# Retention by feature in column tiles, and one product for x by token and the logits

## The chip, the cores and the metric

The kernel runs on one core of one Trainium2 chip. The metric is device time in microseconds (us) of that core. The profile is one execution recorded by the hardware profiler; times inside it count from the first instruction. The engines are PE (TensorE matmul; PEld is its weight load), DVE (VectorE), ACT (ScalarE), POOL (GpSimd) and SP (SyncE, which here only issues transfers).

## What is computed

Retention over 8 sequences of 576 tokens with 8 heads of 64 features, then a mixture of 8 experts in which a local gate can keep the expert of the token before. All data is 32-bit floating point.

```python
scores = scale * np.matmul(q, k.transpose(0, 1, 3, 2))            # q, k, v: (8, 8, 576, 64)
gamma = 1.0 - 2.0 ** (-5.0 - np.arange(H))
Dmat = np.where(rel >= 0, gamma[:, None, None] ** rel[None], 0.0) # rel = query place - key place
x = np.matmul(scores * Dmat, v)                                   # then (B, S, H*D) = (8, 576, 512)
logits = x @ w_gate;  local_gate = sigmoid(x @ w_local)
for each sequence, for each token s:
    e = argmax(logits[s]) if s == 0 or local_gate[s] < 0.5 else the expert of token s - 1
    out[s] = softmax(logits[s])[e] * (relu(x[s] @ w1[e]) @ w2[e]) # w1: (8, 512, 1024), w2: (8, 1024, 512)
```

## The kernel before

**Three stages.** Retention turns q, k and v into x, 128 tokens (a *chunk*) at a time, writes x to DRAM and keeps the logits of both gates. Routing works out on all 4608 tokens which expert each goes to and which slot it gets. The experts' stage gathers x by slot, 256 slots to a block, and sends 25 blocks through their expert's weights. Routing needs the logits of every token, and the address of the first expert's weights needs the routing, so the stages follow one another.

**A chunk of retention.** Two sequences of 576 tokens are nine chunks; the fifth (`m == MID`) ends one sequence and begins the next. The decay is split into a factor by query place and one by key place, so a chunk needs only a triangular mask and a running 64 x 64 state per head. `scores(i)` loads the chunk (`ld`, L107: queries by feature, keys and values by token), transposes the keys on PE (`kps`, L112), copies them on ACT (`kT`, L114), scales the values by key decay on POOL (`vs`, L116), multiplies keys and queries per head (`sps`, L123) and masks the result on DVE (`sT`, L127). The products of L123 have 64 rows of contraction: even heads use partitions 0 to 63, odd heads 64 to 127, in turn. `outputs(i)` adds up in `ops` the chunk's own part (L139, 8 products) and the state's (L146, 4 products), brings the state up to date (`kv` on PE, L155, copied to `state` by ACT, L161), scales `ops` by query decay on DVE (`x`, L163) and stores x (L166). `logits(i)` transposes x (`xps`, L172), copies it on ACT (`xT`, L174) and multiplies it with the gates' weights into `lps` (L176), which is copied once at the end of the stage (`lt`, L187).

**What sets the order.** The program is written as a pipeline: chunk i + 1's scores, chunk i's outputs, chunk i - 1's logits. A scheduler orders each engine's instructions when the program is built, and so the groups of one chunk on PE stand among those of its neighbours. Tiles come from pools with a fixed number of buffers (`raw` 4, `work` 3, `ps_s` 3, `ps_t` 2, `ps_o` and `ps_kv` 1): a tile waits until the reader of the one whose buffer it takes is done. SP issues the loads and the stores of x in its own order; two small tables come over ACT's queue at the start. On PE a 32-bit product is carried out as two passes, each a weight load and a matmul, and shows as two instructions in the profile; a transpose is one.

Of the kernel before, what the change touches and what calls it, by code (L numbers as in the profile page):

```python
# [9 lines left out]
F32 = mybir.dt.float32  # L10
# [9 lines left out]
P = 128  # L20
# [21 lines left out]
def kernel(  # L42
# [3 lines left out]
    decay: bass.AP,  # L46
# [25 lines left out]
    with ExitStack() as part:  # L72
# [26 lines left out]
        lps = ps_l.tile([P, NCH, E + 1], F32, name="lps")  # L99
        chunks = [{} for _ in range(NCH)]  # L100
        kv = None

        def scores(i):
            m = i % PER
            g = chunks[i]
            ld = raw.tile([P, 3, D], F32, name="ld")
            nc.sync.dma_start(out=ld.rearrange("p t x -> p (t x)"), in_=qkv[i])  # L107
            qT = ld[:, 0].rearrange("p (c s) -> p c s", c=HP)
            kn, vn = ld[:, 1], ld[:, 2]
            kps = ps_t.tile([P, HP, P], F32, name="kps", tag="t")  # L110
            for c in range(HP):
                nc.tensor.transpose(kps[:, c, :], kn[:, c * P:(c + 1) * P], ident)  # L112
            kT = work.tile([P, HP, P], F32, name="kT")
            nc.scalar.copy(kT, kps)  # L114
# [3 lines left out]
                dec[:, 1, m, :].unsqueeze(2).to_broadcast([P, H, DH]), op=Alu.mult)  # L118
            sps = [ps_s.tile([P, HP, P], F32, name=f"sps{u}", tag="s") for u in range(2)]
            for c in range(HP):  # L120
                for u in range(2):
                    r = slice(u * DH, (u + 1) * DH)
                    nc.tensor.matmul(sps[u][:, c, :], lhsT=kT[r, c, :], rhs=qT[r, c, :],  # L123
                                     start=True, stop=True, skip_group_check=True)
# [332 lines left out]
```

## Time and profile before

| What | Value |
|---|---|
| Runs | median 1039.18 us of 3 (1037.77 to 1045.94) |
| Profiled execution, first to last instruction | 1037.5 us (its own time is this span; the median of the runs is 1.7 us above it) |
| Busy, share of the span | PE 94%, PEld 69%, DVE 16%, POOL 14%, ACT 12% |
| Granted TensorE clock, mean | 0.977 |
| DMA | 166 MB, 160 GB/s over the span |
| Retention | until 250.83 us, when `lt` is copied |
| Routing | until about 274 us |
| Experts | until the end |

A profile row of the time line has start and busy time in us, the engine, the kernel's line, the operation, output <- inputs, for PE the active rows * columns of the array and the shape of the output, and how many instructions are merged in the row. In a row by group, the numbers after the bar are the sum of busy time in us, the mean of one instruction in ns, and the idle time ahead of the group with what ended it. Matmuls are pipelined: one lasts some 280 ns though the next starts well before that, so what a pass costs is read from start to start.

### The profile page before, as it was taken

Reading aid. Unit: us, or ns where it says so; the run is one execution under the profiler, and the core shown is the slowest. Engines: PE = TensorE matmul, PEld = TensorE weight load, DVE = VectorE, ACT = ScalarE, POOL = GpSimd, SP = SyncE. Lnnn points to the kernel's source line nnn. Section 1 sums busy time; section 2 is a strip of 40 time slices with the busy share of each in tenths; the row PEclk is TensorE's granted clock in tenths of the full one; section 3 lists DMA queues with packets and bytes.
Section 4 is the critical chain, followed back from the end, with each engine's and each line's share of the span. In section 5 each row is a group of like instructions: output and inputs, shape, how many; then the busy total and the mean of one; then the engine's idle time right before and its main releaser. Section 6 shows DMA issues by size and latency. Waiting matters only on the chain. (4 is left out here: it accounts for less than half of the span.)

```text
span 1037.5 us, 12062 instructions
## 1 busy us (share of the span) xinstructions
PE 974.9 (94%) x4918; PEld 719.0 (69%) x4918; DVE 166.8 (16%) x282; ACT 123.8 (12%) x238; POOL 140.7 (14%) x158
## 2 busy tenths in 40 slices
PE   7999999996479999999999999999999999999995
PEld 6999999995466666666666666666666666666662
DVE  2333332324711111010111111010111110010100
ACT  2222222221000000000000000000000000000000
POOL 2111111110021111011111110011111110110000
PEclk9999999998589999999999999999999999999998
DMA  5444444430735544555455544555455544555300
GB/s 201 154 158 157 151 163 162 163 133 32 273 122 203 201 156 148 185 197 177 153 179 187 193 156 153 181 193 188 138 187 203 164 158 160 195 183 167 127 2 0
DMA packets 47509, 166.03 MB, mean 160 GB/s; under 512 B 7006, under 2 KB 7134, under 8 KB 47456
## 3 DMA queue, kind: packets, MB, share of 16 engines
q1 hardware_dynamic: 39168, 142.62, 40.5%
q0 software_dynamic: 8000, 22.56, 6.3%
q8 instruction: 39, 0.64, 0.2%
q14 instruction: 14, 0.11, 0.0%
q10 hardware_dynamic: 288, 0.09, 0.0%
HBM read 146.37 MB, written 22.54 MB: 163 GB/s over the span
## 5 line engine op out<-in xcount | busy, mean ns | idle before, releaser
L395 PE MATMUL hps<-xTs,w1s 128*128 128x256 f32 x1600 | 353.2, 382 | 14.1 <-DVE xTs L389 14.1
L402 PE MATMUL yps<-w2s,hT 128*128 128x512 f32 x800 | 347.4, 592 | 0.0
L395 PEld LDWEIGHTS hps<-xTs,w1s 128*128 128x128 f32 x1600 | 303.0, 191 | 60.2 <-DVE xTs L389 19.8
L402 PEld LDWEIGHTS yps<-w2s,hT 128*128 128x128 f32 x800 | 152.0, 190 | 180.7 <-issue 179.4
L405 DVE TENSOR_SCALAR y<-yps,pslot 128x512 f32<-128x512 f32 x50 | 37.5, 751 | 665.4 <-PE yps L402 665.4
L397 ACT ACTIVATE hT<-hps 128x512 f32<-128x512 f32 x100 | 59.7, 597 | 700.2 <-PE hps L395 700.2
L406 POOL DMA_INDIRECT out_dram<-y,sidx x50 | 50.7, 1014 | 512.0 <-DVE y L405 505.3
L139 PE MATMUL ops<-vs,sT 128*128 128x64 f32 x576 | 82.3, 277 | 0.0
L139 PEld LDWEIGHTS ops<-vs,sT 128*128 128x128 f32 x576 | 72.4, 191 | 4.9 <-issue 0.6
L127 DVE TENSOR_TENSOR sT<-sps,mask 128x512 f32<-128x512 f32 x72 | 46.4, 686 | 159.9 <-PE sps L123 159.9
L383 POOL DMA_INDIRECT xg<-xd,gidx x50 | 48.7, 975 | 164.0 <-PE xgps L388 121.2
L116 POOL TENSOR_TENSOR vs<-ld,dec 128x512 f32<-128x512 f32 x36 | 37.5, 1042 | 190.0 <-PE kv L155 173.2
L123 PE MATMUL sps<-ld,kT 64*128 64x128 f32 x576 | 43.2, 288 | 0.2 <-DVE sT L127 0.2
L161 ACT COPY state<-kv 64x256 f32<-64x256 f32 x64 | 23.4, 366 | 160.2 <-PE kv L155 159.4
L176 PE MATMUL lps<-wg,xT 128*128 128x9 f32 x288 | 38.0, 259 | 1.5 <-ACT xT L174 1.1
L176 PEld LDWEIGHTS lps<-wg,xT 128*128 128x128 f32 x288 | 34.9, 191 | 5.2 <-ACT xT L174 4.7
L123 PEld LDWEIGHTS sps<-ld,kT 64*128 64x128 f32 x576 | 36.3, 190 | 2.9 <-DVE sT L127 0.4
L388 PEld LDWEIGHTS xgps<-ident,xg 128*128 128x128 f32 x200 | 24.2, 146 | 20.1 <-issue 19.5
L155 PE MATMUL kv<-vs,ld 128*128 128x128 f32 (+1 forms) x256 | 35.5, 281 | 0.5 <-ACT state L161 0.5
L146 PE MATMUL ops<-state,ld 128*128 128x128 f32 (+1 forms) x256 | 35.4, 281 | 0.0
L388 PE MATMUL xgps<-ident,xg 128*128 128x128 f32 x200 | 27.7, 282 | 6.6 <-DMA xg<-xd,gidx 6.6
L389 DVE COPY xTs<-xgps 128x512 f32<-128x512 f32 x50 | 32.2, 682 | 7.1 <-PE xgps L388 7.1
(112 smaller groups left out, 271.2 us busy)
## 6 DMA issues: line engine op xcount, KB each, us to landing
w1s<-in_w_dram SPq DMA_DIRECT2D x100, 512.0 KB, 5.5
w2s<-in_w_dram SPq DMA_DIRECT2D x100, 512.0 KB, 8.1
ld<-in_qkv_dram SPq DMA_DIRECT2D x36, 768.0 KB, 4.5
xd<-x SPq DMA_DIRECT2D x36, 256.0 KB, 2.2
xg<-xd,gidx POOLq DMA_INDIRECT x50, 7.3
out_dram<-y,sidx POOLq DMA_INDIRECT x50, 7.5
dec<-in_decay_dram ACTq DMA_DIRECT2D x1, 72.0 KB, 4.6
wg<-in_wgl_dram ACTq DMA_DIRECT2D x1, 18.0 KB, 6.2
```

Source lines behind the costliest of these rows:

```text
L116: nc.gpsimd.tensor_tensor(vs.rearrange("p (h d) -> p h d", h=H), vn.rearrange("p (h d) -> p h d", h=H), dec[:, 1, m, :].unsqueeze(2).to_br ...
L123: nc.tensor.matmul(sps[u][:, c, :], lhsT=kT[r, c, :], rhs=qT[r, c, :], start=True, stop=True, skip_group_check=True)
L127: nc.vector.tensor_tensor(sT[:, u], sps[u], (mask2 if m == MID else mask).unsqueeze(1).to_broadcast([P, HP, P]), op=Alu.mult)
L139: nc.tensor.matmul(ops[:, h, :], lhsT=sT[:, h % 2, h // 2, :], rhs=vs[:, h * DH:(h + 1) * DH], start=(h == 0), stop=(m == 0), skip_group_c ...
L176: nc.tensor.matmul(lps[:, i, :], lhsT=xT[:, c, :], rhs=wg[:, c, :], start=(c == 0), stop=(c == DK - 1), skip_group_check=True)
L383: nc.gpsimd.indirect_dma_start(out=xg, out_offset=None, in_=xd, in_offset=bass.IndirectOffsetOnAxis(ap=gidx[:, s:s + 1], axis=0))
L388: nc.tensor.transpose(xps[:, c, :], xg[:, c * P:(c + 1) * P], ident)
L395: nc.tensor.matmul(hps[:, v, :], lhsT=w1s[:, m + v, c, :], rhs=xT[:, c, :], start=(c == 0), stop=(c == DK - 1), skip_group_check=True)
L397: nc.scalar.activation(hT[:, m:m + 2, :], hps, Act.Relu)
L402: nc.tensor.matmul(yps, lhsT=hT[:, m, u * P:(u + 1) * P], rhs=w2s[:, m, :], start=(m == 0), stop=(m == FK - 1))
L405: nc.vector.tensor_scalar(y, yps, pslot[:, s:s + 1], None, Alu.mult)
L406: nc.gpsimd.indirect_dma_start(out=out, out_offset=bass.IndirectOffsetOnAxis(ap=sidx[:, s:s + 1], axis=0), in_=y, in_offset=None, bounds_c ...
```

## The change

`ops` is computed the other way round, by feature instead of by token: the values are the stationary operand with 64 columns, the masked scores stream, and even and odd heads write partitions 0 to 63 and 64 to 127, that is, they use the left and the right 64 columns of the array (L163 of the changed kernel). The state's part of `ops` is turned round in the same way (L144). `kv` is computed per head in 64 columns each instead of per pair of heads in 128 (L154), without the products between different heads, which were thrown away. x therefore comes out by feature (`xT`, L168, scaled by a table of query decay by feature and place, `decq`, of 1280 KB instead of a small one). One product per 128 features with the matrix [identity, gates' weights] (`gates`, 137 columns) then gives x by token and that part of the logits at once (`nps`, L175); ACT copies x out (L178), DVE sums the logits' four parts into `lt` (L179), and x is stored (L181). Keys are loaded in both layouts, so that `ld` grows from 768 to 1024 KB and their transposes and copies go.

```diff
-        ps_t = pool(part, "ps_t", 2, PSUM)
         ps_s = pool(part, "ps_s", 3, PSUM)
-        ps_o = pool(part, "ps_o", 1, PSUM)
+        ps_o = pool(part, "ps_o", 2, PSUM)
+        ps_n = pool(part, "ps_n", 1, PSUM)
         ps_kv = pool(part, "ps_kv", 1, PSUM)
-        ps_l = pool(part, "ps_l", 1, PSUM)
...
-        dec = once.tile([P, 2, PER, H], F32, name="dec")
-        nc.scalar.dma_start(out=dec.rearrange("p t m h -> p (t m h)"), in_=decay)
-        wg = once.tile([P, DK, E + 1], F32, name="wg")
-        nc.scalar.dma_start(out=wg.rearrange("p k e -> p (k e)"), in_=wgl)
+        deck = once.tile([P, PER, H], F32, name="deck")
+        nc.scalar.dma_start(out=deck.rearrange("p m h -> p (m h)"), in_=decay_k)
+        gates = once.tile([P, DK, P + E + 1], F32, name="gates")
+        nc.scalar.dma_start(out=gates[:, :, P:], in_=wgl.rearrange("p (k e) -> p k e", k=DK))
+        decq = once.tile([P, HP, S + HALF], F32, name="decq")
+        nc.scalar.dma_start(out=decq.rearrange("p c s -> p (c s)"), in_=decay_q)
+        for c in range(DK):
+            nc.gpsimd.tensor_copy(gates[:, c, 0:P], ident)
...
+        def half(u):
+            return slice(u * DH, (u + 1) * DH)
...
         def scores(i):
-            ld = raw.tile([P, 3, D], F32, name="ld")
+            ld = raw.tile([P, 4, D], F32, name="ld")
             nc.sync.dma_start(out=ld.rearrange("p t x -> p (t x)"), in_=qkv[i])
             qT = ld[:, 0].rearrange("p (c s) -> p c s", c=HP)
-            kn, vn = ld[:, 1], ld[:, 2]
-            kps = ps_t.tile([P, HP, P], F32, name="kps", tag="t")
-            for c in range(HP):
-                nc.tensor.transpose(kps[:, c, :], kn[:, c * P:(c + 1) * P], ident)
-            kT = work.tile([P, HP, P], F32, name="kT")
-            nc.scalar.copy(kT, kps)
+            kT = ld[:, 1].rearrange("p (c s) -> p c s", c=HP)
+            kn, vn = ld[:, 2], ld[:, 3]
...
         def outputs(i):
-            ops = ps_o.tile([P, H, DH], F32, name="ops")
-            for h in range(H):
-                nc.tensor.matmul(ops[:, h, :], lhsT=sT[:, h % 2, h // 2, :],
-                                 rhs=vs[:, h * DH:(h + 1) * DH],
-                                 start=(h == 0), stop=(m == 0), skip_group_check=True)
+            ops = ps_o.tile([P, HP, P], F32, name="ops")
             if m > 0:
                 n = HALF if m == MID else P
                 for c in range(HP):
-                    nc.tensor.matmul(
-                        ops[0:n, 2 * c:2 * c + 2, :].rearrange("p h d -> p (h d)"),
-                        lhsT=qT[:, c, 0:n], rhs=states[(i + 1) % 2][:, c, :],
-                        start=False, stop=True, skip_group_check=True)
+                    nc.tensor.matmul(ops[:, c, 0:n], lhsT=states[(i + 1) % 2][:, c, :],
+                                     rhs=qT[:, c, 0:n], start=(c == 0), stop=False,
+                                     skip_group_check=True)
             if m != PER - 1:
                 r = slice(HALF, P) if m == MID else slice(0, P)
                 if m in (0, MID):
-                    kv = ps_kv.tile([P, HP, P], F32, name="kv")
+                    kv = ps_kv.tile([P, HP, DH], F32, name="kv")
                 for c in range(HP):
-                    nc.tensor.matmul(kv[:, c, :], lhsT=kn[r, c * P:(c + 1) * P],
-                                     rhs=vs[r, c * P:(c + 1) * P],
-                                     start=(m in (0, MID) and c == 0), stop=True,
-                                     skip_group_check=True)
+                    for u in range(2):
+                        h = 2 * c + u
+                        nc.tensor.matmul(kv[half(u), c, :], lhsT=kn[r, h * DH:(h + 1) * DH],
+                                         rhs=vs[r, h * DH:(h + 1) * DH],
+                                         start=(m in (0, MID) and c == 0), stop=True,
+                                         skip_group_check=True)
                 for u in range(2):
-                    r = slice(u * DH, (u + 1) * DH)
-                    nc.scalar.copy(states[i % 2][r, :, r], kv[r, :, r])
-            g["x"] = x = work.tile([P, D], F32, name="x")
-            nc.vector.tensor_tensor(
-                x.rearrange("p (h d) -> p h d", h=H), ops,
-                dec[:, 0, m, :].unsqueeze(2).to_broadcast([P, H, DH]), op=Alu.mult)
-            nc.sync.dma_start(out=xd[i * P:(i + 1) * P, :], in_=x)
+                    nc.scalar.copy(states[i % 2][half(u), :, half(u)], kv[half(u)])
+            for c in range(HP):
+                for u in range(2):
+                    h = 2 * c + u
+                    nc.tensor.matmul(ops[half(u), c, :], lhsT=vs[:, h * DH:(h + 1) * DH],
+                                     rhs=sT[:, u, c, :], start=(m == 0 and c == 0), stop=True,
+                                     skip_group_check=True)
+            g["xT"] = xT = work.tile([P, HP, P], F32, name="xT")
+            at = (m * P) % S
+            nc.vector.tensor_tensor(xT, ops, decq[:, :, at:at + P], op=Alu.mult)
...
-        def logits(i):
-            x = chunks[i]["x"]
-            xps = ps_t.tile([P, DK, P], F32, name="xps", tag="t")
-            for c in range(DK):
-                nc.tensor.transpose(xps[:, c, :], x[:, c * P:(c + 1) * P], ident)
-            xT = work.tile([P, DK, P], F32, name="xT")
-            nc.scalar.copy(xT, xps)
-            for c in range(DK):
-                nc.tensor.matmul(lps[:, i, :], lhsT=xT[:, c, :], rhs=wg[:, c, :],
-                                 start=(c == 0), stop=(c == DK - 1), skip_group_check=True)
+        def by_token(i):
+            xT = chunks[i]["xT"]
+            nps = ps_n.tile([P, DK, 2 * P], F32, name="nps")
+            for c in range(DK):
+                nc.tensor.matmul(nps[:, c, 0:P + E + 1], lhsT=xT[:, c, :], rhs=gates[:, c, :],
+                                 start=True, stop=True, skip_group_check=True)
+            x = work.tile([P, DK, P], F32, name="x")
+            nc.scalar.copy(x, nps[:, :, 0:P])
+            nc.vector.tensor_reduce(lt[:, i, :], nps[:, :, P:P + E + 1].rearrange("p k e -> p e k"),
+                                    axis=AX.X, op=Alu.add)
+            nc.sync.dma_start(out=xd[i * P:(i + 1) * P, :], in_=x.rearrange("p k d -> p (k d)"))
...
             if i > 0:
-                logits(i - 1)
-        nc.vector.tensor_copy(lt, lps)
+                by_token(i - 1)
```

On the host side the arrays change to match: `qkv` holds the keys twice, and the decay table becomes one by key place and one by feature and query place.

In the middle of the stage, PE's rows for one chunk are these before (names with a number are one buffer of a tile; `sps` alternates between two tiles for four products each, of which the first two are shown, and `x4` counts products):

```order
L139 MATMUL ops<-vs,sT 128x64 x2
L146 MATMUL ops<-state_108,ld 128x128 x4
L155 MATMUL kv<-vs,ld 128x128 x4
L172 MATMUL xps<-ident,x 128x128 x4
L112 MATMUL kps<-ident,ld 128x128 x4
L139 MATMUL ops<-vs,sT 128x64 x3
L176 MATMUL lps<-wg,xT 128x9 x4
L139 MATMUL ops<-vs,sT 128x64 x3
L123 MATMUL sps_1039<-ld,kT 128x128
L123 MATMUL sps_1040<-ld,kT 128x128
```

In the changed program PE's rows for one chunk at the same place are these:

```order
L144 MATMUL ops<-ld,state_112 128x128 x4
L154 MATMUL kv<-vs,ld 64x64 x8
L163 MATMUL ops<-sT,vs 64x128 x8
L175 MATMUL nps<-gates,xT 128x137 x4
L125 MATMUL sps_1171<-ld 128x128
L125 MATMUL sps_1172<-ld 128x128
```

The transposes and the logits' products are gone, `nps` of the chunk before stands behind `ops`, and the groups stand whole, in the order of the code, where three groups of `ops` lay between others.

At the start of the program PE has these rows before, with what each waits for (a DMA's landing, or another engine):

```order
L112 MATMUL kps<-ident,ld 128x128 [waits DMAHW1_49,Pool_49]
L112 MATMUL kps<-ident,ld 128x128 x3
L112 MATMUL kps<-ident,ld 128x128 [waits DMAHW3_49]
L112 MATMUL kps<-ident,ld 128x128 x3
L155 MATMUL kv<-vs,ld 128x128 [waits Pool_49]
L155 MATMUL kv<-vs,ld 128x128 x2
L123 MATMUL sps_124<-ld,kT 128x128 [waits Activation_49]
```

And these in the changed program, where the rows left out are the other products of the first two chunks' scores:

```order
L125 MATMUL sps_119<-ld 128x128 [waits DMAHW1_49]
L125 MATMUL sps_120<-ld 128x128
L125 MATMUL sps_136<-ld 128x128 [waits DMAHW4_49]
L125 MATMUL sps_137<-ld 128x128 [waits DVE_49]
L154 MATMUL kv<-vs,ld 64x64 [waits Pool_49]
L163 MATMUL ops<-sT,vs 64x128
```

The scores wait for the load alone and come first, where they stood behind two chunks' transposes and ACT's copies.

SP's queue in the middle of the stage, before:

```order
L107 DMA ld<-in_qkv_dram 128x1536 [waits DMAHW0_49,DMAHW1_49,PE_49,Pool_49]
L166 DMA xd<-x 128x512 [waits DVE_49]
L166 DMA xd<-x 128x512 [waits DMAHW2_49,DVE_49]
L107 DMA ld<-in_qkv_dram 128x1536 [waits DMAHW3_49,PE_49,Pool_49]
L166 DMA xd<-x 128x512 [waits DMAHW4_49,DVE_49]
```

And in the changed program:

```order
L181 DMA xd<-x 128x512 [waits DMAHW1_49,Activation_49]
L114 DMA ld<-in_qkv_dram 128x2048 [waits DMAHW2_49,PE_49,Pool_49]
L181 DMA xd<-x 128x512 [waits DMAHW3_49,Activation_49]
L114 DMA ld<-in_qkv_dram 128x2048 [waits DMAHW4_49,PE_49,Pool_49]
L181 DMA xd<-x 128x512 [waits DMAHW5_49,Activation_49]
```

Loads and stores still take turns; the store waits for ACT's copy instead of DVE's product, and a load for PE and POOL to be done with the chunk whose buffer it takes.

More of the change, by code (lines that the diff above doesn't have):

```diff
@@ L45 @@
     qkv: bass.AP,
-    decay: bass.AP,
+    decay_k: bass.AP,
+    decay_q: bass.AP,
     wgl: bass.AP,
@@ L117, in scores @@
                 vs.rearrange("p (h d) -> p h d", h=H), vn.rearrange("p (h d) -> p h d", h=H),
-                dec[:, 1, m, :].unsqueeze(2).to_broadcast([P, H, DH]), op=Alu.mult)
+                deck[:, m, :].unsqueeze(2).to_broadcast([P, H, DH]), op=Alu.mult)
             sps = [ps_s.tile([P, HP, P], F32, name=f"sps{u}", tag="s") for u in range(2)]
@@ L121, in scores @@
                 for u in range(2):
-                    r = slice(u * DH, (u + 1) * DH)
-                    nc.tensor.matmul(sps[u][:, c, :], lhsT=kT[r, c, :], rhs=qT[r, c, :],
+                    nc.tensor.matmul(sps[u][:, c, :], lhsT=kT[half(u), c, :], rhs=qT[half(u), c, :],
                                      start=True, stop=True, skip_group_check=True)
@@ L419, in _by_feature, with _decays @@
     return x.transpose(0, 3, 2, 1).reshape(NCH, P, D)
[L422 to L424 removed]
+def _decays(np):
     gamma = 1.0 - 2.0 ** (-5.0 - np.arange(H))
[L426 to L428 removed]
+    at = ((np.arange(PER)[None, :] * P + np.arange(P)[:, None]) % S).astype(np.float64)
+    k = gamma[None, None, :] ** -at[:, :, None]
+    at = (np.arange(S + HALF) % S).astype(np.float64)
+    head = 2 * np.arange(HP)[None, :] + np.arange(P)[:, None] // DH
+    q = gamma[head][:, :, None] ** at / math.sqrt(DH)
+    return k.reshape(P, PER * H).astype(np.float32), q.reshape(P, HP * (S + HALF)).astype(np.float32)
 def kernel(**inputs):
```

16 lines of the change are left out of this document (6 added, 10 removed).

## The prediction

> **What bounds the kernel now.** I read the busy shares by stage first, then the order of TensorE's groups inside one chunk, then the waits. The first fence is the profile's first line; the second is the table by stretch (columns: stretch, its length, busy us of PE, PEld, DVE, ACT and POOL, granted clock, DMA share, GB/s).
>
> ```profile
> PE 974.9 (94%) x4918; PEld 719.0 (69%) x4918; DVE 166.8 (16%) x282; ACT 123.8 (12%) x238; POOL 140.7 (14%) x158
> ```
>
> ```profile
> 105.47:165.15 59.68, 59.55 (x562) 56.35 (x561) 17.73 (x27) 15.52 (x34) 9.38 (x9) 1.00 0.48 160
> 250.83:274.11 23.28, 1.73 (x6) 0.68 (x6) 20.74 (x59) 0.44 (x1) 2.10 (x10) 0.50 0.31 108
> 274.11:1037.50 763.39, 731.57 (x2672) 490.38 (x2672) 73.61 (x114) 59.70 (x100) 99.43 (x100) 0.99 0.48 164
> ```
>
> Retention fills the first 250.83 us with PE never idle (59.55 of 59.68 us), routing 23 us on DVE, the experts the rest. The change touches retention alone; what follows it keeps its instructions, so 1037.5 - 250.83 us stay. Inside retention, one engine is full and PE's own instructions set the time. Here is one chunk on PE (start us, busy us, group, passes):
>
> ```profile
> 102.67 0.60 PE L112 MATMUL kps<-ident,ld 128*128 128x128 f32 x4
> 103.11 0.78 PE L139 MATMUL ops<-vs,sT 128*128 128x64 f32 x6
> 103.76 1.06 PE L176 MATMUL lps<-wg,xT 128*128 128x9 f32 x8
> 104.68 0.86 PE L139 MATMUL ops<-vs,sT 128*128 128x64 f32 x6
> 105.47 1.16 PE L123 MATMUL sps<-ld,kT 64*128 64x128 f32 x16
> 106.56 0.66 PE L139 MATMUL ops<-vs,sT 128*128 128x64 f32 x4
> 107.06 1.11 PE L146 MATMUL ops<-state,ld 128*128 128x128 f32 x8
> 108.00 1.06 PE L155 MATMUL kv<-vs,ld 128*128 128x128 f32 x8
> 108.89 0.60 PE L172 MATMUL xps<-ident,x 128*128 128x128 f32 x4
> 109.33 0.60 PE L112 MATMUL kps<-ident,ld 128*128 128x128 f32 x4
> ```
>
> A product of the program is two passes here (8 `ops` products are 16), a transpose one. From start to start a pass costs 0.111 us (`kv`: 0.89/8; `kps`: 0.44/4) whether 128, 64 or 9 columns stream. **The exception** is `sps`: its 16 passes, on 64 rows each in two row halves, take 1.09 us, so two passes share one slot of 0.111 us (8 x 0.111 = 0.89) and 0.20 us is left for going back to the full array; going in costs 0.79 - 6 x 0.111 = 0.12. So a switch of the array's shape costs about 0.16 us. The chunk is 48 x 0.111 + 0.89 + 2 x 0.16 = 6.54 us against 6.66 between the two `kps` rows; the rest is this wait (us in total, times, longest):
>
> ```profile
> PEld lps L176 <- ACT xT L174: 3.6, 21, 0.5
> ```
>
> Nine chunks (one pair of sequences) run from the `sps` at 105.47 to this one, 59.68 us, 6.63 each:
>
> ```profile
> 165.15 1.16 PE L123 MATMUL sps<-ld,kT 64*128 64x128 f32 x16
> ```
>
> **The change part by part.** Gone from each chunk: 4 `kps` and 4 `xps` transposes, 8 `lps` passes. New: 8 `nps` passes. `ops` and `kv` become 16 passes each with 64 weight columns, alternating between the two column halves of the array. No row of before has two column halves at work. The nearest are the fifth chunk's (the one with two sequences):
>
> ```profile
> 100.08 1.09 PE L146 MATMUL ops<-state,ld 128*64 128x128 f32 x8
> 101.10 1.16 PE L155 MATMUL kv<-vs,ld 64*128 64x128 f32 x8
> 102.18 0.55 PE L172 MATMUL xps<-ident,x 128*128 128x128 f32 x3
> ```
>
> ```profile
> 100.08 0.19 PEld L146 LDWEIGHTS ops<-state,ld 128*64 128x64 f32 x2
> ```
>
> ```profile
> L146 PEld LDWEIGHTS ops<-state,ld 128*64 128x64 f32 x32 | 3.4, 136 | 0.3
> L146 PE MATMUL ops<-state,ld 128*64 128x128 f32 x32 | 4.3, 279 | 0.0
> ```
>
> ```profile
> 103.11 0.33 PE L139 MATMUL ops<-vs,sT 128*128 128x64 f32 x2
> ```
>
> ```profile
> L139 PE MATMUL ops<-vs,sT 128*128 128x64 f32 x576 | 82.3, 277 | 0.0
> ```
>
> One column half alone keeps the 0.111 us (1.02 us for 8 with a switch of 0.13; the next 8 on a row half take 1.08, a switch of 0.19). Two loads of 64 columns follow each other at 0.19 - 0.136 = 0.055 us, and two passes of 64 streamed columns with their weights ready at 0.33 - 0.277 = 0.053.
>
> - `ops`, 128 streamed columns: 16 passes between 8 x 0.111 = 0.89 us (halves side by side, as `sps` does) and 16 x 0.111 = 1.78. I take 0.89, the row of two tiles at work being nearest. By the Trainium skill, TensorE: Matmul & The Clock Gate, Measured speedup vs the span model, three column tiles gave 2.38 times, not 3. By that ratio a pair would cost an estimated 0.140 us and the whole time 12 us more; the `sps` rows show a full factor of two for row halves, and no run here shows column halves.
> - `kv`, 64 streamed columns: between 8 x 0.055 = 0.44 and 16 x 0.111 = 1.78. I take 0.44, since load and pass of this very width have those two rows; 0.89 (a pair per slot of 0.111) is the middle case.
> - `nps`, 137 streamed columns. The experts' 256 columns give the slope:
>
> ```profile
> L395 PE MATMUL hps<-xTs,w1s 128*128 128x256 f32 x1600 | 353.2, 382 | 14.1 <-DVE xTs L389 14.1
> ```
>
>   353.2/1600 = 0.221, so 0.111 + 9 x 0.110/128 = 0.119, and 8 x 0.119 = 0.95 us (bounds 0.89 to 1.77, nearest the lower).
> - Switches: row halves, full, column halves, full: 4 instead of 2, at 0.13 to 0.19.
>
> An ordinary chunk is then 0.89 (`sps`) + 0.89 (state) + 0.44 + 0.89 + 0.95 + 4 x 0.16 = **4.70 us**. Of nine, the first has no state product and a switch less (3.65), the fifth a switch more for its `kv` on 64 x 64 (4.86), the last no `kv` (4.26): 6 x 4.70 + 12.77 = 40.97, or 4.55 each. Against 59.68 that is 18.71 us per nine, and over the 33 periods between the third and the last `sps` **68.6 us**.
>
> What hides the rest. In the stretch of nine above DVE has 17.73 us, ACT 15.52 and POOL 9.38. DVE gains a small reduce per chunk, of 36 elements a partition, between nothing and the 0.45 us of this row with 288; ACT loses one copy of this kind:
>
> ```profile
> 251.03 0.45 DVE L227 TENSOR_REDUCE mx<-lt 128x36 f32<-128x288 f32 x1 [0.19 <-DVE lt L187]
> ```
>
> ```profile
> L174 ACT COPY xT<-xps 128x512 f32<-128x512 f32 x32 | 18.7, 585 | 14.2 <-PE xps L172 13.5
> ```
>
> DVE needs at most 2.4 us and ACT 1.2 of 4.55, so both stay hidden. On DVE the reduce waits for ACT's copy of the same `nps`; behind it stand the masks of the next scores, which cannot start until PE has done the next `sps`, 1.05 us with its switch, so it delays about nothing. On SP the store of `x` now waits for ACT; behind it stands a load, which itself must wait for the next chunk's `kv`. It is issued more than two chunks (over 9 us) before its use and landed in this time (the last column, us):
>
> ```profile
> ld<-in_qkv_dram SPq DMA_DIRECT2D x36, 768.0 KB, 4.5
> ```
>
> The start and the end of the stage, before:
>
> ```profile
> 5.34 1.09 PE L112 MATMUL kps<-ident,ld 128*128 128x128 f32 x4 [5.34 <-DMA ld<-in_qkv_dram]
> ...
> 7.26 1.12 PE L112 MATMUL kps<-ident,ld 128*128 128x128 f32 x4 [0.84 <-DMA ld<-in_qkv_dram]
> ...
> 9.15 1.04 POOL L116 TENSOR_TENSOR vs<-ld,dec 128x512 f32<-128x512 f32 x1 [0.74 <-DMA ld<-in_qkv_dram]
> ```
>
> ```profile
> 17.60 1.16 PE L123 MATMUL sps<-ld,kT 64*128 64x128 f32 x16
> ```
>
> ```profile
> 238.45 1.16 PE L123 MATMUL sps<-ld,kT 64*128 64x128 f32 x16
> ...
> 250.34 0.49 DVE L187 COPY lt<-lps 128x324 f32<-128x324 f32 x1 [3.57 <-PE lps L176]
> ```
>
> Loads land 1.9 us apart, 404 KB/us. The third of the larger loads, with all 1280 KB of `decq` ahead of it, lands at 3.4 + (3 x 1024 + 1280)/404 = 14.2 us, where the third `sps` stood at 17.60: **3.4 us** gained (some 2 more if `decq` comes behind, an estimate; 0 if PE's cold first groups bind as before). After the last `sps`, the same prices leave one ordinary chunk without its first switch (4.54) and state, switch, `ops`, switch and `nps` of the last (3.05), 7.59 us up to the last but one `nps`. Since `nps` has one buffer, the last waits for ACT's copy and the reduce: twice (0.17 for a pass to end, 279 ns less its slot, + 0.59 + 0.3) + 0.95 + an estimated 0.35 in hand-offs gives 11.0 against 12.38 us: **1.3 us**.
>
> Sum: 68.6 + 3.4 + 1.3 = 73.3 us off the profiled 1037.5, 964.2. The runs' median, 1039.18, stands 1.7 us above that span, so I forecast **966 us**.
>
> **Rivals.**
> 1. *Loads bind.* DMA was busy 0.48 of 6.63 us per chunk, 3.2 us for 1024 KB; 1280 KB (1.31 MB) need 4.0 of 4.55. The fullest stretch shows a share of 0.85 at 311 GB/s:
>
> ```profile
> 270.00:300.00 30.00, 19.32 (x101) 17.62 (x102) 12.09 (x20) 0.00 (x0) 6.85 (x7) 0.65 0.85 311
> ```
>
>   At 311 GB/s a chunk takes 4.21 us; were it a tenth slower, 4.7, adding 0.13 x 36 = 5, and with stalls about 975 us.
> 2. *The change does not get its overlap*: column halves take turns. `ops` +0.89 x 36, `kv` +0.44 x 32: 46 us back, 1012. For it: one PE, one stream of instructions. Against: `sps`.
> 3. *No gain at all*: every pass keeps its slot of 0.111. `ops` +32, `kv` +1.34 x 32 = 43: 1041.
> 4. *Slower.* A weight load cannot run under a pass that uses the same rows, and all column-half passes use all 128. Place: the 16 + 16 passes per chunk. Price: 0.136 + 0.111 us for a pass of `ops`, 0.136 + 0.055 for one of `kv`: 3.95 - 0.89 and 3.06 - 0.44 us more, 194 us in all, 1160. It decides from 0.110 us per pass on: 73.3 us over 36 x 16 + 32 x 16 = 1088 passes is 0.067 above my mean of 0.042. Against it: the eight `L146` passes on one column half, 128 rows each, took 1.02 us, not 8 x 0.247. The rule is the Trainium skill's, TensorE: Matmul & The Clock Gate, Part 3: Packing small matmuls — row/col tiling: loads overlap passes in flight only where the row groups differ; the trace disagrees with it for one half, and no run here shows it for two.
>
> **How the numbers follow.** Forecast 0.72, loads 0.10, turns 0.08, no gain 0.04, slower 0.06. The forecast's own bounds: `kv` at 0.89 adds 0.45 x 32 = 14; switches 4 x 0.03 x 36 = 4 either way; a start without gain adds 3, with `decq` last takes 2; the unexplained 0.12 us per chunk adds 4. That is 960 to 991; with the loads' stalls, and 3 us for the scatter of the runs, 957 to 1000, which holds 0.82. What a measurement tells here from no change is 1%, 10 us: faster by more 0.90 (forecast, loads, turns), within 0.04, slower by more 0.06.
>
> **What would show it.** Right: groups of 16 `ops` passes starting 0.89 us before the next group less a switch; nine chunks in about 41 us; PE still full; no PE wait for `ld`, `nps` or `xT`. Wrong: `ops` at 1.8 us (turns or no gain), PE waiting for `ld` (loads), `kv` near 0.9 us (the small term missized), or a stretch after 250 us that changes though its instructions do not.

## The result, and the profile after

| | before | changed |
|---|---|---|
| Runs, median (lowest to highest), us | 1039.33 (1037.77 to 1045.94), 4 runs | **967.84** (966.20 to 968.47), 4 runs |
| Profiled execution, span, us | 1037.5 | 964.5 |
| Granted TensorE clock, mean | 0.977 | 0.981 |
| Ratio of the times | | **0.9306** (95% interval 0.9276 to 0.9336) |

The forecast was 966 us in a range of 957 to 1000. A later run (chip 7) gave 967.25 (966.21 to 968.59, 6 runs), ratio 0.9296 (0.9265 to 0.9327).

The changed kernel's stretches (columns: stretch, length, busy us of PE, PEld, DVE, ACT and POOL, granted clock, DMA share, GB/s): nine chunks, routing, experts.

```profile
28.93:70.73 41.80, 41.80 (x554) 36.99 (x553) 19.59 (x36) 11.15 (x25) 9.02 (x10) 1.00 0.83 283
179.83:202.53 22.70, 1.74 (x6) 0.67 (x6) 20.35 (x57) 0.44 (x1) 1.18 (x7) 0.57 0.35 118
202.53:964.50 761.97, 729.53 (x2672) 488.90 (x2672) 73.63 (x114) 59.72 (x100) 99.63 (x100) 0.99 0.48 165
```

The nine chunks take 41.80 us where they took 59.68. PE is still full in them, while the DMA share rose from 0.48 to 0.83. PE's share of the whole hardly moved (94 to 93%): in retention it does less work in less time, which no share of the span shows. The last two stretches begin at the same places as those of before, the last logits and PE's first `slots` product (L351, L348 before), which follows routing: routing takes 22.70 us where it took 23.28, the experts 762.0 where they took 763.4.

One ordinary chunk on PE's time line (start, busy us, group, passes):

```profile
102.92 1.16 PE L125 MATMUL sps<-ld 64*128 64x128 f32 x16
104.01 1.16 PE L144 MATMUL ops<-ld,state 128*128 128x128 f32 x8
105.10 0.69 PE L154 MATMUL kv<-vs,ld 128*64 128x64 f32 x16
105.61 1.05 PE L163 MATMUL ops<-sT,vs 128*64 128x128 f32 x16
106.59 1.21 PE L175 MATMUL nps<-gates,xT 128*128 128x137 f32 x8
107.72 1.16 PE L125 MATMUL sps<-ld 64*128 64x128 f32 x16
```

From start to start: `sps` 1.09, state 1.09, `kv` 0.51, `ops` 0.98, `nps` 1.13, together 4.80 us. The 16 column-half passes of `ops` take hardly more than the 8 slots of 0.111 of one half, and those of `kv` half as long: both halves of the array work at once.

The start and the end of the stage, on the same time line and on DVE's:

```profile
5.84 2.08 PE L125 MATMUL sps<-ld 64*128 64x128 f32 x16 [5.84 <-DMA ld<-in_qkv_dram]
8.41 2.67 PE L125 MATMUL sps<-ld 64*128 64x128 f32 x16 [0.49 <-DMA ld<-in_qkv_dram]
...
13.13 1.16 PE L125 MATMUL sps<-ld 64*128 64x128 f32 x16
...
18.18 1.21 PE L175 MATMUL nps<-gates,xT 128*128 128x137 f32 x8 [1.31 <-DVE xT L168]
```

```profile
17.43 0.69 DVE L168 TENSOR_TENSOR xT<-ops,decq 128x512 f32<-128x512 f32 x1 [5.45 <-DMA decq<-in_decay_q_dram]
```

```profile
168.84 1.16 PE L125 MATMUL sps<-ld 64*128 64x128 f32 x16
...
177.72 1.21 PE L175 MATMUL nps<-gates,xT 128*128 128x137 f32 x8 [0.95 <-DVE lt L179]
```

```profile
179.63 0.20 DVE L179 TENSOR_REDUCE lt<-nps 128x9 f32<-128x36 f32 x1 [0.53 <-ACT x L178]
```

The third `sps` stands at 13.13 us (17.60 before), the last at 168.84 (238.45), and the last logits are there at 179.83 (250.83). Once the first load is there, PE waits three times in the whole of retention: 0.49 us for the second load; 1.31 us shortly before the fourth scores, for `xT`, which DVE could not write before `decq` had landed; and 0.95 us at the end, for the single buffer of `nps`. A load of 1024 KB lands 6.9 us after its issue (the median); this is the one of `decq` (KB, us from issue to landing):

```profile
decq<-in_decay_q_dram ACTq DMA_DIRECT2D x1, 1280.0 KB, 15.4
```

### The profile page after: what moved, and what is told of

Its sections match the earlier page's. It is cut to its first block, busy times and chain, and to the rows that moved or that the text cites. A ratio compares the mean times of both kernels' runs of the same rounds, so it can differ in the third digit from the quotient of the medians.

```text
span 964.5 us, 11954 instructions
## 1 busy us (share of the span) xinstructions
PE 901.6 (93%) x4886; PEld 640.3 (66%) x4886; DVE 173.2 (18%) x317; ACT 106.0 (11%) x202; POOL 141.4 (15%) x162
## 5 line engine op out<-in xcount | busy, mean ns | idle before, releaser
L119 POOL TENSOR_TENSOR vs<-ld,deck 128x512 f32<-128x512 f32 x36 | 37.6, 1044 | 123.6 <-DMA ld<-in_qkv_dram 94.2
L125 PE MATMUL sps<-ld 64*128 64x128 f32 x576 | 44.2, 293 | 6.3 <-DMA ld<-in_qkv_dram 6.3
L175 PE MATMUL nps<-gates,xT 128*128 128x137 f32 x288 | 43.4, 292 | 2.3 <-DVE xT L168 1.3
L125 PEld LDWEIGHTS sps<-ld 64*128 64x128 f32 x576 | 37.1, 195 | 11.2 <-DMA ld<-in_qkv_dram 6.6
L175 PEld LDWEIGHTS nps<-gates,xT 128*128 128x128 f32 x288 | 36.1, 189 | 8.5 <-issue 5.3
L163 PE MATMUL ops<-sT,vs 128*64 128x128 f32 x576 | 38.3, 275 | 0.0
L144 PE MATMUL ops<-ld,state 128*128 128x128 f32 (+1 forms) x256 | 36.7, 286 | 0.0
L144 PEld LDWEIGHTS ops<-ld,state 128*128 128x128 f32 x256 | 31.0, 191 | 3.8
L168 DVE TENSOR_TENSOR xT<-ops,decq 128x512 f32<-128x512 f32 x36 | 24.9, 691 | 45.3 <-PE ops L163 39.9
## 6 DMA issues: line engine op xcount, KB each, us to landing
decq<-in_decay_q_dram ACTq DMA_DIRECT2D x1, 1280.0 KB, 15.4
```

What stands on the lines that cost most here:

```text
L119: nc.gpsimd.tensor_tensor(vs.rearrange("p (h d) -> p h d", h=H), vn.rearrange("p (h d) -> p h d", h=H), deck[:, m, :].unsqueeze(2).to_broa ...
L125: nc.tensor.matmul(sps[u][:, c, :], lhsT=kT[half(u), c, :], rhs=qT[half(u), c, :], start=True, stop=True, skip_group_check=True)
L144: nc.tensor.matmul(ops[:, c, 0:n], lhsT=states[(i + 1) % 2][:, c, :], rhs=qT[:, c, 0:n], start=(c == 0), stop=False, skip_group_check=True)
L163: nc.tensor.matmul(ops[half(u), c, :], lhsT=vs[:, h * DH:(h + 1) * DH], rhs=sT[:, u, c, :], start=(m == 0 and c == 0), stop=True, skip_gro ...
L175: nc.tensor.matmul(nps[:, c, 0:P + E + 1], lhsT=xT[:, c, :], rhs=gates[:, c, :], start=True, stop=True, skip_group_check=True)
```

## The experiments

The theory: TensorE sets the time of retention, a pass costs its slot, two passes on two halves of the array share one, and a change of the array's shape costs something under 0.2 us; loads and other engines are hidden. Diffs are against the changed kernel, but for the last two runs, which are against the kernel before; `...` stands for lines left out.

**1. The halves not in turn.** All even heads first, then all odd heads, in `kv` and `ops`:

```diff
-                for c in range(HP):
-                    for u in range(2):
+                for u in range(2):
+                    for c in range(HP):
...
```

> The same products of ops and kv, but all four on the left 64 columns first and then all four on the right, instead of in turn. If the gain on ops and kv comes from two column halves at work in the same slot, they now run one after the other: 16 passes of ops at 0.109 us instead of 8 slots (+0.87 us in 36 chunks), 16 of kv at 0.057 (+0.45 in 32), +45 us on the 967.8 of the changed kernel, about 1012 us. Rival: the gain comes from 64 columns of weights being shorter to load, or the array looks ahead far enough to pair them whatever their order; then 968 us within 5.

Measured: 987.55 us (986.76 to 989.42), ratio 0.9483 (0.9433 to 0.9533). It lost 20 us, not 45, and not the 5 at most of the rival either. An ordinary chunk takes 5.40 us. On PE's time line `ops`, here in a chunk without `kv`, takes 1.51 us up to `nps` (first fence), and in the next chunk the first pass of `ops` starts ahead of the last passes of `kv` (second fence):

```profile
101.56 1.58 PE L163 MATMUL ops<-sT,vs 128*64 128x128 f32 x16
103.07 1.21 PE L175 MATMUL nps<-gates,xT 128*128 128x137 f32 x8
```

```profile
105.30 0.79 PE L154 MATMUL kv<-vs,ld 128*64 128x64 f32 x13
105.87 0.32 PE L163 MATMUL ops<-sT,vs 128*64 128x128 f32 x1
105.92 0.28 PE L154 MATMUL kv<-vs,ld 128*64 128x64 f32 x2
```

So the halves need not be issued in turn to overlap: PE starts a pass on an idle half some passes ahead of its place. In the `ops` of the first fence the right half's first pass starts beside the left half's fifth, 0.49 us behind its start. Between 0.98 us (all overlapped) and about 1.9 (none, experiment 4) it reaches about halfway. The theory's premise, that only neighbours overlap, was wrong; that the overlap carries the gain stood.

**2. `kv` as before**, four products of 128 columns that are half thrown away:

```diff
-                    for u in range(2):
-                        h = 2 * c + u
-                        nc.tensor.matmul(kv[half(u), c, :], lhsT=kn[r, h * DH:(h + 1) * DH],
-                                         rhs=vs[r, h * DH:(h + 1) * DH],
...
+                    nc.tensor.matmul(kv[:, c, :], lhsT=kn[r, c * P:(c + 1) * P],
+                                     rhs=vs[r, c * P:(c + 1) * P],
...
```

> The changed kernel with kv as before: per pair of heads, 128 columns of weights, 128 columns streaming, four products. The order and the number of switches stay. Theory: 8 slots of 0.111 us instead of 8 of 0.058, +0.43 us in 32 chunks, +14 us, 981 us. Rival (the pairs of kv are already hidden beside other work, or PE is not the bound there because loads are): 968 us within 3.

Measured: 980.57 us (980.06 to 982.16), ratio 0.9414 (0.9364 to 0.9463), as expected. On PE `kv` now takes 0.98 us instead of 0.51. The switch that stood ahead of it stands behind it, which makes the state's product 0.09 us shorter and `ops` 0.05 longer, so an ordinary chunk takes 5.23 us:

```profile
107.30 1.06 PE L152 MATMUL kv<-vs,ld 128*128 128x128 f32 x8
108.28 1.09 PE L161 MATMUL ops<-sT,vs 128*64 128x128 f32 x16
```

**3. x by token and the logits apart**, four transposes and four products with the gates' 9 columns:

```diff
-                nc.tensor.matmul(nps[:, c, 0:P + E + 1], lhsT=xT[:, c, :], rhs=gates[:, c, :],
-                                 start=True, stop=True, skip_group_check=True)
+                nc.tensor.transpose(nps[:, 0, c, :], xT[:, c, :], ident)
+            for c in range(DK):
+                nc.tensor.matmul(nps[:, 1, 0, 0:E + 1], lhsT=xT[:, c, :], rhs=gates[:, c, P:],
...
```

> The changed kernel with the one product of 137 columns taken apart: four transposes of xT (one pass each, 0.111 us) and four products with the gates' 9 columns (8 passes of 0.111), added up in PSUM; DVE copies nine logits instead of reducing 36. Theory: 12 slots of 0.111 = 1.33 us instead of 8 of 0.118 = 0.94, +0.39 us in 36 chunks, +14 us, 982 us. Rival (a product with identity costs more than a transpose, so that nothing is won by the merge): 968 us or less.

Measured: 976.23 us (975.99 to 977.45), ratio 0.9367 (0.9319 to 0.9416): 8.4 us lost instead of 14. On PE:

```profile
103.33 0.66 PE L175 MATMUL nps<-ident,xT 128*128 128x128 f32 x4
103.83 0.96 PE L177 MATMUL nps<-gates,xT 128*128 128x9 f32 x8
104.71 1.16 PE L125 MATMUL sps<-ld 64*128 64x128 f32 x16
```

1.38 us for 12 passes is 12 x 0.111 + 0.05, where the one product leaves 1.13 - 0.95 = 0.18 beside its slots. So the four slots come as priced, and the smaller rest gives a part back. It is not that the switch behind passes of 9 columns is cheap: the next `sps` starts 0.19 us behind their last pass, 0.07 over a slot, much as behind 137 columns (0.21). But the second of these passes starts only 0.03 us behind the first, 0.08 under a slot, and the transposes lose 0.05 at their start.

**4. One half alone.** The odd heads' products of `ops` also write the left half, in 28 of the 36 chunks. There the left half's results hold both heads' sums, and the right half's lack their own part.

```diff
-                    nc.tensor.matmul(ops[half(u), c, :], lhsT=vs[:, h * DH:(h + 1) * DH],
+                    nc.tensor.matmul(ops[half(u if m in (0, MID) else 0), c, :], lhsT=vs[:, h * DH:(h + 1) * DH],
```

> In 28 of the 36 chunks (all but the first and the fifth of each pair of sequences) the odd heads' products of ops are added to the left 64 columns too, so that the right half's come out without that part; as many passes of the same size, all on one column half. Theory: nothing can pair, 16 passes of 0.109 us instead of 8 slots, +0.87 us in 28 chunks, +24 us, 992 us. Rival (the gain on ops is that of the shorter weight load or of the stream's turn, not of two halves side by side): 968 us within 3.

Measured: 991.78 us (990.43 to 991.81), ratio 0.9517 (0.9464 to 0.9571), as expected. On PE the same 16 passes take 1.89 us instead of 0.98:

```profile
103.46 1.96 PE L163 MATMUL ops<-sT,vs 128*64 128x128 f32 x16
105.35 1.21 PE L175 MATMUL nps<-gates,xT 128*128 128x137 f32 x8
```

With nothing else changed, the second half of the array is worth 24 us in `ops` alone.

**5. A load of 1536 KB**, whose last 512 KB nothing reads:

```diff
-            ld = raw.tile([P, 4, D], F32, name="ld")
+            ld = raw.tile([P, 6, D], F32, name="ld")
...
```

> The changed kernel with two more copies of the values in each chunk's load, which nothing reads: 1536 KB instead of 1024. Theory: DMA is busy 0.83 of a chunk's 4.81 us now, with 1024 + 256 KB; 1792 KB need 0.83 x 4.81 x 1792/1280 = 5.6 us, so loads bind and a chunk takes 5.4 to 5.6 us: +21 to +28 us over 36 chunks, and some 4 us at the start, 993 to 1000 us, with PE waiting for ld. Rival (DMA's busy share overstates, descriptors overlap): 968 within 5.

Measured: 994.94 us (993.20 to 997.01), ratio 0.9554 (0.9502 to 0.9607). The time is as expected, its make-up is not. PE's waits from 5 to 200 us (total, times, longest), the stretch from 40 to 140 us, and PE's order in a part of the chunks:

```profile
PE sps L125 <- DMA ld<-in_qkv_dram: 11.4, 9, 7.7
PE nps L175 <- DVE xT L168: 10.6, 1, 10.6
```

```profile
40.00:140.00 100.00, 96.11 (x1196) 82.60 (x1198) 42.05 (x79) 24.20 (x54) 18.79 (x18) 1.00 0.93 347
```

```profile
67.48 0.50 PE L175 MATMUL nps<-gates,xT 128*128 128x137 f32 x2
67.91 0.43 PE L163 MATMUL ops<-sT,vs 128*64 128x128 f32 x2
```

7.7 us are the first load (5.84 in the changed kernel), and 10.6 us are one wait for `xT` and so for `decq`, which lands behind the first loads; in the 4.8 us behind that wait the granted clock is 0.58. From the fourth `sps` to the last a chunk takes 5.19 us on average, against 4.67 in the changed kernel, 17 us in all; but between 33 and 200 us PE waits only 3.6 us for loads, and 2.7 us for the buffer of `nps`. In the rest PE is busy at a clock of 1.00, but in another order: in a part of the chunks `nps` and `ops` stand in pieces between each other, with more switches. So the expected time came by luck, and the run does not show a chunk bound by loads. Nor is 347 GB/s the most that DMA reaches: it moved 415 GB/s from 5.84 to 13.13 us of the changed kernel.

Even at 347 GB/s the changed kernel's 1.31 MB a chunk need 3.8 of its 4.80 us: hidden, with a fifth to spare.

**6. One switch less.** The state's product moves from ahead of `kv` to behind `ops`, so that the full array's two groups (state, `nps`) are neighbours:

```diff
-            if m > 0:
-                n = HALF if m == MID else P
-                for c in range(HP):
-                    nc.tensor.matmul(ops[:, c, 0:n], lhsT=states[(i + 1) % 2][:, c, :],
...
+            if m > 0:
+                n = HALF if m == MID else P
+                for c in range(HP):
+                    nc.tensor.matmul(ops[:, c, 0:n], lhsT=states[(i + 1) % 2][:, c, :],
...
```

> The changed kernel with the state's product of ops moved behind the column-half products, next to nps, which uses the full array too: row halves, column halves, full array, three switches of the array's shape per chunk instead of four (no change in each sequence pair's first chunk). Same products and bytes. Theory: a switch costs 0.20 us as the changed kernel's rows show, so -0.20 in 32 chunks, -6.4 us, 961.5 us. Rival 1 (a switch's price lies in waiting for the products in flight, which the next group of another tile would wait for anyway): no change, 968. Rival 2 (loads bind): less than half of it, since DMA's share of 0.83 would rise to 0.87.

Measured: **960.98** us (960.75 to 962.76), ratio 0.9238 (0.9207 to 0.9268), as expected. On PE:

```profile
104.85 1.16 PE L125 MATMUL sps<-ld 64*128 64x128 f32 x16
...
107.43 1.16 PE L163 MATMUL ops<-ld,state 128*128 128x128 f32 x8
108.43 1.11 PE L175 MATMUL nps<-gates,xT 128*128 128x137 f32 x8
109.47 0.72 PE L125 MATMUL sps<-ld 64*128 64x128 f32 x8
```

The same passes take 4.62 us from `sps` to `sps` instead of 4.80: this switch cost 0.18 us.

**7. One switch more.** `by_token` of the chunk before is called between `kv` and `ops`:

```diff
+            if i > 0:
+                by_token(i - 1)
             for c in range(HP):
                 for u in range(2):
                     h = 2 * c + u
                     nc.tensor.matmul(ops[half(u), c, :], lhsT=vs[:, h * DH:(h + 1) * DH],
...
-            if i > 0:
+            else:
                 by_token(i - 1)
```

> The changed kernel with nps moved between kv and ops: full array, column halves, full array, column halves, row halves, five switches per chunk instead of four (four instead of three in each pair's first chunk, three instead of four in its last). Same products and bytes. Theory: +0.20 in 28 + 4 - 4 chunks, +5.6 us, 973.5 us. Rival (switches are free or hidden): 968.

Measured: 971.64 us (970.24 to 972.94), ratio 0.9337 (0.9305 to 0.9369), 4.4 us slower than the changed kernel on the same chip. The direction is right and the size a little below what was expected:

```profile
103.87 0.69 PE L154 MATMUL kv<-vs,ld 128*64 128x64 f32 x16
104.48 1.21 PE L177 MATMUL nps<-gates,xT 128*128 128x137 f32 x8
105.62 1.09 PE L165 MATMUL ops<-sT,vs 128*64 128x128 f32 x16
106.64 1.16 PE L125 MATMUL sps<-ld 64*128 64x128 f32 x16
```

From `kv` to `sps` 2.77 us stand against 2.62 in the changed kernel, 0.15 more: 0.10 in `kv`, 0.04 in `ops` and 0.01 in `nps`.

**8. One switch less, and `decq` for the first chunk first**, as a tile of its own of 256 KB, on top of the move of experiment 6:

```diff
+        decq0 = once.tile([P, HP, P], F32, name="decq0")
+        nc.scalar.dma_start(out=decq0, in_=decay_q.rearrange("p (c s) -> p c s", c=HP)[:, :, 0:P])
...
-            nc.vector.tensor_tensor(xT, ops, decq[:, :, at:at + P], op=Alu.mult)
+            nc.vector.tensor_tensor(xT, ops, decq0 if i == 0 else decq[:, :, at:at + P], op=Alu.mult)
```

> The three switches, and the first chunk's part of the query decay (256 KB) in a tile of its own that is loaded ahead of the whole table. Theory: the wait of 1.3 us of the first nps for xT goes, and the 0.2 us of later ones; -6.4 - 1.4 us, 960 us. Rival (the 256 KB delay the first loads by as much): as with three switches alone.

Measured: **960.40** us (959.04 to 961.47), ratio 0.9230 (0.9198 to 0.9261), the shortest of all. The profiled span is 1.4 us shorter than that of experiment 6 (958.0 against 959.4) and the wait for `xT` is gone, but the medians differ by 0.6 us, inside the runs' scatter: the gain is seen in the trace and not in the times.

**9. The keys alone.** The kernel before, with the keys loaded in both layouts:

```diff
-            ld = raw.tile([P, 3, D], F32, name="ld")
+            ld = raw.tile([P, 4, D], F32, name="ld")
...
-            kps = ps_t.tile([P, HP, P], F32, name="kps", tag="t")
-            for c in range(HP):
-                nc.tensor.transpose(kps[:, c, :], kn[:, c * P:(c + 1) * P], ident)
-            kT = work.tile([P, HP, P], F32, name="kT")
-            nc.scalar.copy(kT, kps)
+            kT = ld[:, 1].rearrange("p (c s) -> p c s", c=HP)
...
```

> The kernel before with the keys loaded in both layouts and nothing else changed: no key transposes, no ACT copies of them, loads of 1024 KB. The scheduler now puts the logits' products in the middle of the scores, so that a chunk has four switches of the array's shape instead of two. Theory: 4 passes of 0.111 us and the wait for ACT's copy go (-0.44 - 0.12 us), two switches of 0.20 come (+0.40): about -0.1 to -0.2 us per chunk, and some 4 us at the start: 1028 to 1034 us. Rival (key transposes are the main gain, switches hidden): 36 x 0.56 + 4 = -24 us, 1015 us.

Measured: **1066.34** us (1060.73 to 1068.92), ratio 1.0220 (1.0155 to 1.0284). Work was taken away and the kernel is slower, by 1.6 to 2.8%; theory and rival, which both made it faster, were wrong. PE's time line has an ordinary chunk and the beginning of a slow one; below it the waits at `lps` of PE's weight loads and of PE itself from 20 to 220 us, and two stretches:

```profile
53.00 2.00 PE L135 MATMUL ops<-vs,sT 128*128 128x64 f32 x16
...
57.21 0.72 PE L119 MATMUL sps<-ld 64*128 64x128 f32 x8
58.35 1.06 PE L172 MATMUL lps<-wg,xT 128*128 128x9 f32 x8 [0.43 <-ACT xT L170]
59.34 0.71 PE L119 MATMUL sps<-ld 64*128 64x128 f32 x8
59.98 3.03 PE L135 MATMUL ops<-vs,sT 128*128 128x64 f32 x16
```

```profile
PEld lps L172 <- ACT xT L170: 13.8, 25, 0.9
PE lps L172 <- ACT xT L170: 8.7, 21, 0.7
```

```profile
5.00:272.00 267.00, 255.15 (x2029) 235.52 (x2030) 69.91 (x106) 42.02 (x95) 37.83 (x38) 0.90 0.49 172
62.00:64.00 2.00, 2.00 (x11) 2.00 (x11) 0.00 (x0) 0.00 (x0) 0.00 (x0) 0.50 0.00 0
```

Without the keys' transposes the scheduler put the logits' products into the middle of the scores, right behind the transposes of x whose copy they need. In 25 chunks their weight loads waited, up to 0.9 us, and in 21 PE itself, up to 0.7, the scores' shape was left and entered twice, and the granted clock fell to 0.50 for stretches at a time: the same 16 passes of L135 take 2.00 us and 3.03. A mean clock of 0.90 instead of the 1.00 of the kernel before (5 to 250 us) is an estimated 27 us over 267. At full clock, too, the chunk is long: 6.98 us from the L135 at 53.00 to the one at 59.98.

**10. The same without the wait.** On top of experiment 9's edit, the logits' products come one step of the pipeline later, when ACT has long copied x:

```diff
-        for i in range(NCH + 1):
+        for i in range(NCH + 2):
...
+            if i > 1:
+                products(i - 2)
...
```

> The kernel before with the keys loaded in both layouts (1024 KB per chunk, no transposes and copies of the keys), as in the run before that was slower than the kernel before, but with the logits' products of a chunk one step of the pipeline later, so that ACT's copy of x is long done when they come. My theory: that run lost its time because these products stood in the middle of the scores, waited up to 0.9 us for ACT in each chunk, and the granted clock fell to half after such gaps. Then PE has no wait here, the clock in retention is as in the kernel before (1.00 in mid-stage), and a chunk is 44 passes of 0.111 (8 state, 8 kv, 16 ops, 4 transposes of x, 8 logits) + 0.89 for the scores + about 0.35 for two switches = 6.13 us against 6.63: 0.5 x 36 = 18 us, and some 4 us at the start, so 1015 to 1020 us. Rival: the larger load, or the missing transposes between the groups, slow PE by themselves: then it stays at 1045 or above, at a clock below 0.95 in retention without gaps, or with waits for the load.

Measured: **1013.55** us (1012.95 to 1014.40), ratio 0.9758 (0.9741 to 0.9774), just below what was expected. The stretch from 40 to 140 us, and a chunk:

```profile
40.00:140.00 100.00, 100.00 (x986) 97.16 (x985) 33.17 (x51) 20.97 (x47) 17.74 (x17) 1.00 0.65 224
```

```profile
100.98 1.16 PE L119 MATMUL sps<-ld 64*128 64x128 f32 x16
102.07 2.00 PE L135 MATMUL ops<-vs,sT 128*128 128x64 f32 x16
...
107.07 1.16 PE L119 MATMUL sps<-ld 64*128 64x128 f32 x16
```

PE is full, the clock is 1.00 and the chunk takes 6.09 us: 0.89 less than in experiment 9 at full clock, 32 us in 36 chunks. With the 27 us of the clock that is 6 more than the 53 us between the two; the counts overlap, since not every chunk of experiment 9 waits. The same loads and the same missing transposes gain 26 us once no product waits, so neither was to blame: the place of the logits' products was. The move takes away the waits and two of four switches at once; but the changed kernel has four switches in a chunk and a clock of 1.00, so switches alone do not lower it. The run also splits the change: about 26 us come with the keys, given that later place, and the other 46 (1013.55 to 967.25) with the column halves and the joint product.

## Why the prediction was right

**The bound.** Read rightly: PE's groups set the chunk, and every run that changed a group's passes moved the time by about that amount times the chunks that it touched (`kv` 0.42 x 32 = 13 us, `ops` on one half 0.91 x 28 = 25).

**`ops` at 0.89 and `kv` at 0.44.** Chosen from bounds that reached to 1.78; measured 0.98 and 0.51 with the ends of the groups included. The second half is worth nearly a factor of two: 1.89 us on one half, 0.98 on two. The ratio of 2.38 for three column tiles from the Trainium skill's TensorE: Matmul & The Clock Gate, Measured speedup vs the span model, does not carry over to two halves here. The rival that made the kernel slower rested on Part 3 of the same page of the Trainium skill: weight loads overlap only passes on other rows. The trace disagrees on both forms of it, since column-half passes share all 128 rows and yet start every 0.06 us (0.98/16) on two halves and every 0.12 (1.89/16) on one. "Turns" was wrong twice over: the halves overlap even when they are not issued in turn (experiment 1).

**`nps`.** Forecast 0.95 by its slope, measured 1.13 with its switch; experiment 3 confirms the four slots saved.

**Switches, the term that was mis-sized.** Four were to cost 0.64 us, 0.16 each, read from the two of the kernel before. The groups above exceed their slots by 0.20 (`sps`), 0.20 (state), 0.07 (`kv`), 0.09 (`ops`) and 0.18 (`nps`), 0.74 in all. Hence a chunk of 4.80 instead of 4.70 and nine in 41.80 instead of 40.97. From the third to the last `sps` 65.1 us were saved ((238.45 - 17.60) - (168.84 - 13.13)) instead of 68.6; the wait of 1.31 us for `xT` lies in this stretch too. Experiments 6 and 7 price a switch alone, at 0.18 and 0.15: inside the bounds of 0.13 to 0.19, one above and one below the value taken.

**The start.** Forecast 3.4, measured 4.5 (17.60 to 13.13). `decq` did not land ahead of the loads but behind them, 15.4 us after its issue; the prediction had priced that case at some 2 us more. What it left out is that DVE then waits for `decq`, and PE for DVE, 1.31 us, behind the third `sps`.

**The tail.** 179.83 - 168.84 = 10.99 us, forecast 11.0, with the wait for the one buffer of `nps` that it named.

**The sum.** 65.1 + 4.5 + 1.4 = 71.0 us of retention against 73.3. The span fell by 73.0; the other 2.0 us lie behind retention, where the instructions are those of before: 0.6 in routing and 1.4 in the experts, whose first 26 us have a granted clock of 0.78 where it was 0.67. A change there was among the prediction's signs of being wrong; why it came is not shown. That the forecast span of 964.2 us stands 0.3 from the measured one is therefore in part luck: retention alone missed by 2.3.

**Loads.** Hidden, as forecast: no PE wait for a load behind the second, at 283 GB/s. The 311 GB/s that the prediction took for its rival were no end of DMA's, which moved 347 GB/s in mid-stage of experiment 5 and 415 at the start of the changed kernel.

**Not foreseen.** The prediction treated the keys' part as eight slots less with nothing of its own to lose. Alone it loses 27 us (experiment 9). In the changed kernel the joint product comes a whole chunk behind `xT`, and PE waits for nothing in mid-stage. The sum holds, but it never asked whether the new order keeps PE without gaps and so its clock, and a part that could lose 27 us stood in it as a sure gain.

## What to carry to other kernels

Where a full TensorE sets the time, count slots from start to start and changes of the array's shape: two products of 64 columns side by side cost as much as one, and groups of one shape belong next to each other (6 us for moving one product). Removing work from a full engine can expose a dependence that the work covered; look in the new order for what now stands right behind its own producer.

## What the runs showed of the hardware that was not expected

- A pass on an idle column half starts several passes ahead of its turn (experiment 1: 1.51 us for 16 passes issued half after half, against 0.98 in turn and 1.89 on one half).
- What a change of shape costs goes, in these rows, with the group that it leads to and not with what streamed before it. Single passes show it; the first two rows are the changed kernel's, the others experiment 7's:

```profile
104.89 0.28 PE L144 MATMUL ops<-ld,state 128*128 128x128 f32 x1
106.81 0.40 PE L175 MATMUL nps<-gates,xT 128*128 128x137 f32 x2
```

```profile
104.33 0.22 PE L154 MATMUL kv<-vs,ld 128*64 128x64 f32 x1
105.78 0.39 PE L165 MATMUL ops<-sT,vs 128*64 128x128 f32 x4
```

To leave a group costs about 0.09 us over its slot: `kv` starts 0.21 us behind the state's last pass (104.89 to 105.10), and `nps` 0.15 behind the last of `kv` (104.33 to 104.48), whose pairs follow each other at 0.06. To enter one costs 0.10 for `nps` (its second pass 0.22 behind its first, 106.59 to 106.81) and 0.05 for `ops` behind it (0.16, 105.62 to 105.78). Experiment 6 saves leaving one group and entering one of the full array, by these rows 0.19 us; experiment 7 adds leaving `kv` and entering `ops`, 0.14. Measured were 0.18 and 0.15. By the Trainium skill, TensorEngine Tiling (Array Packing), Key Properties, a change of tiling mode drains TensorE; the trace agrees in that the next group's first pass comes 0.09 us late each time.
- The granted clock fell to 0.50 with PE waiting no longer than 0.7 us at a time in mid-stage, 8.7 us in 21 waits (experiment 9), and stayed at 1.00 when these waits were removed (experiment 10). The Trainium skill's TensorE: Matmul & The Clock Gate tells of both: its section Why this matters for your kernels warns of idle gaps above about 3 us, which none here reached, and its section A second HAM failure mode: psum-queue depth-cycling of frequent short idling, which fits. In the kernel before, the weight loads wait at this place too, 21 times and up to 0.5 us, but PE itself only once from 20 to 220 us, for 0.3 us, and it keeps its clock; that the waits lower the clock is argued, and where the threshold lies stays open.
- A load of 1280 KB on ACT's queue took 15.4 us beside SP's loads of 1024 KB, which landed in 6.9 us each; split off and issued first, 256 KB of it were in time for the first chunk.
